# Attention and feed-forward with cached keys: each key and value tile loaded in two transfers from two queues

## The chip, the cores and the metric

The kernel runs on one core of one Trainium2 chip. Five engines share the work: PE (TensorE, the matrix engine), DVE (VectorE), ACT (ScalarE), POOL (GpSimd) and SP (SyncE, which here only issues transfers). Sixteen DMA engines carry data between the chip's main memory (HBM) and the on-chip memory (SBUF, 128 partitions). An engine works off its instructions in order, and so does a queue of transfers; between engines, and between transfers and engines, semaphores set the order. The metric is the time of one execution on the device in microseconds (us), as a median of several runs.

## The reference

One decoding step for four sequences (B = 4): a layer norm with a modulation computed from a condition c, attention of one query over 4096 cached keys and values for each of 32 heads of 128 numbers, a projection, a second modulated layer norm, and a feed-forward block with SiLU. All numbers are 32-bit floats.

```
mod = (silu(c) @ w_mod) split into sa, ca, ga, sb, cb, gb
h = layernorm(x) * (1 + ca) + sa
q = (h @ wq) split into 32 heads
scores = (q . k_cache) / sqrt(128)          # k_cache: [4, 32, 4096, 128]
p = softmax(scores)
o = (p . v_cache) @ wo                      # v_cache: [4, 32, 4096, 128]
x = x + ga * o
h = layernorm(x) * (1 + cb) + sb
x = x + gb * (silu(h @ w1) @ w2)
```

The two caches have 268 MB each; every number in them is read once, and is used in one multiplication and one addition. The weights together have 31 MB.

## The kernel before, in words

**Tiles.** The caches are worked through in N = 32 steps. A step n takes four heads of one sequence (t, b = divmod(n, 4): head group t of eight, sequence b): a key tile k_n and a value tile v_n of 128 partitions x 128 rows x 128 numbers, 8.39 MB each, 64 KB in each partition. A head's 4096 rows lie on 32 partitions, 128 rows in each, so that a tile is one stretch of HBM and each partition's 64 KB a stretch of it.

**Buffers.** All tiles and all large weights share three SBUF buffers of one tile each (the pool kv, L63), which are handed out in the order of the program: w_mod, wq, k0, v0, k1, v1, k2 and so on to k31, v31, wo, and w1 with w2. So k_{n+1} takes the buffer of v_{n-1}, and v_{n+1} that of k_n. A transfer waits at its issue until the last instruction that reads the old content is done.

**One step** (L419 to L472). GpSimd multiplies rows 0 to 39 of each partition's keys by the query (mult, L286, from a copy qw of the query in SBUF), VectorE rows 40 to 127 (from qb, the query in PSUM, the matrix engine's memory). VectorE sums both products over the 128 numbers (red, L291) to the scores. The row maxima go over PE (bmax, L299) and VectorE (negmax, L304 to L307); ScalarE takes the exponential (softexp, L313), and GpSimd puts the result in the layout that PE wants (pz, L317). Then the values: GpSimd multiplies rows 0 to 31 by their weights and adds them in halves (vmult, L329 and L333), and PE takes rows 32 to 127 (pv, L354) and later what GpSimd has left (vsum, L339). vsum of step n - 1 runs in step n: it is the last reader of v_{n-1}, and so what releases the buffer of k_{n+1}. The last reader of k_n is red. Every second step VectorE, ScalarE and PE gather the sums of two steps (gather, L368 to L378).

**Queries.** make_qb(n + 1) makes the query for the next step. At each fourth n it first builds four of them with ScalarE (L275) and PE (L277); always it copies one to SBUF with ScalarE (qw, L281).

**Order.** The program is written out by hand: each engine runs its instructions in the order of the text. All transfers are issued by SyncE through one helper (fetch, L85). Of step n, SyncE issues k_{n+1} and then v_{n+1}. Eight completion semaphores go round over the transfers, and a transfer waits for the one eight places before it to land.

**The end.** In step 31 k31 comes in two transfers by halves of its rows, wo (L426) goes into the buffer of v30, and w1 and w2 (L460) into that of k31, in ten transfers. Then follow the projection (project, L412), the second layer norm, and the feed-forward block with its last matmuls at L514.

Of the kernel before, what the change touches and what calls it, by code (L numbers as in the profile page):

```python
# [17 lines left out]
def kernel(  # L18
# [13 lines left out]
    nc = tc.nc  # L32
# [13 lines left out]
    NJ = HP * S // P  # L46
# [12 lines left out]
    N = B * NT  # L59
# [8 lines left out]
    def psum(shape, tag, bufs):  # L68
        return ps.tile(shape, F32, tag=tag, name=tag, bufs=bufs)
# [15 lines left out]
    def fetch(t, src, *cuts):  # L85
        for lo, hi in zip(cuts, cuts[1:]):
            nc.sync.dma_start(t[:, lo:hi], src[:, lo:hi])

    kt, vt = {}, {}

    def load(dst, cache, name, n, *cuts):
        t, b = divmod(n, B)
        dst[n] = Slot(f"{name}{n}").take(NJ, Dh)
        src = cache[b, HP * t : HP * (t + 1)].rearrange("h (p j) d -> (h p) j d", p=QW)
        fetch(dst[n], src, *(cuts or (0, NJ)))

    def load_k(n, *cuts):
        load(kt, kc, "k", n, *cuts)

    def load_v(n):  # L100
        load(vt, vc, "v", n)
# [169 lines left out]
    def make_qb(n):  # L271
        if n % B == 0:
            m = work.tile([P, B, Dh], F32, tag="o", name=f"qm{n}", bufs=1)
            for b in range(B):
                nc.scalar.activation(m[:, b, :], qn, AF.Copy, scale=sel[:, n + b : n + b + 1])  # L275
            p = psum([P, B, Dh], "q", 2)
            nc.tensor.matmul(p, blk.rearrange("p i x -> p (i x)"), m, start=True, stop=True)  # L277
            for b in range(B):
                qb[n + b] = p[:, b, :]
        qw[n] = work.tile([P, Dh], F32, tag="qw", name=f"qw{n}")  # L280
        nc.scalar.activation(qw[n], qb[n], AF.Copy)  # L281
# [3 lines left out]
    def mult(eng, src, n, lo, hi):  # L285
        eng.tensor_mul(  # L286
            kt[n][:, lo:hi, :], kt[n][:, lo:hi, :], src[n].unsqueeze(1).to_broadcast([P, hi - lo, Dh])
        )

    def red(n, lo, hi):  # L290
        nc.vector.tensor_reduce(sc[n][:, lo:hi], kt[n][:, lo:hi, :], axis=AX.X, op=ALU.add)  # L291

    def rowmax(n):
        nm[n] = work.tile([P, 1], F32, tag="rm", name=f"rm{n}")
        nc.vector.tensor_reduce(nm[n], sc[n], axis=AX.X, op=ALU.max)  # L295

    def bmax(n):
        p = psum([P, P], "mx", 2)
        nc.tensor.transpose(p, nm[n].to_broadcast([P, P]), ident)  # L299
        nm[n] = p  # L300

    def negmax(n):
        m = work.tile([P, HP], F32, tag="hx", name=f"hx{n}")
        nc.vector.tensor_reduce(m, nm[n].rearrange("p (i x) -> p i x", i=HP), axis=AX.X, op=ALU.max)  # L304
        nc.vector.tensor_mul(m, m, hn)
        nm[n] = work.tile([P, 1], F32, tag="nm", name=f"nm{n}")
        nc.vector.tensor_reduce(nm[n], m, axis=AX.X, op=ALU.add)  # L307

    def softexp(n):
        t, b = divmod(n, B)  # L310
        if b == 0:
            rs[t] = work.tile([P, B], F32, tag="rs", name=f"rs{t}")
        nc.scalar.activation(sc[n], sc[n], AF.Exp, bias=nm[n], accum_out=rs[t][:, b : b + 1])  # L313
        for h in range(2):
            f = first(n) if h == 0 else 0
            m = HG - f
            nc.gpsimd.tensor_mul(  # L317
                pz[h][:, f * W : HG * W].rearrange("p (g x) -> p g x", g=m)[:, :, E:].rearrange("p g (i j) -> p g i j", i=HP),
                sc[n][:, JJ * (HG * h + f) : HG * JJ * (h + 1)].rearrange("p (g j) -> p g j", j=JJ)
                .unsqueeze(2).to_broadcast([P, m, HP, JJ]),  # L320
                hm.unsqueeze(1).unsqueeze(3).to_broadcast([P, m, HP, JJ]),
            )

    def first(n):
        return NV // JJ if n < N - 2 else 0

    def vmult(n):
        if first(n):
            nc.gpsimd.tensor_mul(  # L329
                vt[n][:, :NV, :], vt[n][:, :NV, :], sc[n][:, :NV].unsqueeze(2).to_broadcast([P, NV, Dh])  # L330
            )
            for m in (NV // 2, NV // 4, JJ):
                nc.gpsimd.tensor_add(vt[n][:, :m, :], vt[n][:, :m, :], vt[n][:, m : 2 * m, :])  # L333

    def vsum(n):
        t, b = divmod(n, B)
        q, a = divmod(b, 2)
        o = (1 - a) * E
        nc.tensor.matmul(  # L339
            po[t, q][0:W, :], hs[:, o : o + W], vt[n][:, :JJ, :].rearrange("p j d -> p (j d)"),  # L340
            start=False, stop=a == 1,
        )

    def pv(n):
        t, b = divmod(n, B)
        q, a = divmod(b, 2)
        if a == 0:
            po[t, q] = psum([P, JJ * Dh], "po", 2)
        f = first(n)
        for j in range(f, NG):  # L350
            g = j % G
            h, u = divmod(j, HG)
            o = u * W + (1 - a) * E
            nc.tensor.matmul(  # L354
                po[t, q][W * g : W * (g + 1), :],
                pz[h][:, o : o + W],
                vt[n][:, JJ * j : JJ * (j + 1), :].rearrange("p j d -> p (j d)"),
                start=(a == 0 and j < f + G), stop=(a == 1 and j >= NG - G and (g > 0 or not f)),
            )
# [24 lines left out]
    def norm(t):  # L384
        p = psum([P, B], "mx", 2)
        g = part(t)
        nc.tensor.matmul(p[g], b8.rearrange("p i x -> p (i x)"), rs[t], start=True, stop=True)
        rd[t] = work.tile([P, B, QA], F32, tag="ra", name="ra", bufs=1)
        m = work.tile([P, B], F32, tag="dx", name="dx")
        nc.vector.reciprocal(m[g], p[g])  # L390
        nc.vector.tensor_mul(
            rd[t][g], m[g].unsqueeze(2).to_broadcast([W, B, QA]), dqm[g].unsqueeze(1).to_broadcast([W, B, QA])
        )

    def spread(t, lo=0, hi=B):
        g, n = part(t), hi - lo
        v = work.tile([P, n, QA, RA], F32, tag="o", name="v", bufs=1)
        nc.vector.tensor_mul(
            v[g], od[t][g, lo:hi, :].rearrange("p b (q r) -> p b q r", q=QA),
            rd[t][g, lo:hi, :].unsqueeze(3).to_broadcast([W, n, QA, RA]),  # L400
        )
        nc.vector.tensor_reduce(
            oo[t // TA][g, :, lo:hi], v[g].rearrange("p b q r -> p r b q"), axis=AX.X, op=ALU.add
        )
# [13 lines left out]
    load_v(0)  # L418
    for n in range(N):  # L419
        t, b = divmod(n, B)  # L420
        if n < N - 2:
            load_k(n + 1)
        elif n == N - 2:
            load_k(n + 1, 0, NJ // 2, NJ)
        else:
            so = Slot("wo")  # L426
            wat, wbt = so.take(RA, D), so.take(RA, D)
            fetch(wat, wav, 0, RA)
            fetch(wbt, wbv, 0, RA - 7, RA - 1, RA)
        sc[n] = work.tile([P, NJ], F32, tag="sc", name=f"sc{n}")  # L430
        if n + 1 < N:
            mult(nc.gpsimd, qw, n, 0, NA)
            mult(nc.vector, qb, n, NA, NJ)
            make_qb(n + 1)
            if n and first(n - 1):
                vsum(n - 1)
            red(n, NA, NJ)
        else:
            mid = NJ // 2
            for lo in (0, mid):  # L440
                mult(nc.gpsimd, qw, n, lo, lo + NH)
            for lo in (0, mid):
                mult(nc.vector, qb, n, lo + NH, lo + mid)
                red(n, lo + NH, lo + mid)
            for j in range(NH):
                nc.scalar.activation(kt[n][:, j, :], kt[n][:, j, :], AF.Copy, accum_out=sc[n][:, j : j + 1])
        if n + 1 < N:
            red(n, 0, NA)
        else:
            red(n, mid, mid + NH)  # L450
        rowmax(n)
        bmax(n)
        negmax(n)
        if t and b == 1:
            spread(t - 1)
        softexp(n)
        if n + 1 < N:
            load_v(n + 1)
        else:
            s2 = Slot("w12")  # L460
            w1t = s2.take(NK, F)
            w2t = s2.take(NI, D)
            fetch(w1t, w1v, 0, 3, 4)
            fetch(w2t, w2v, 0, 6, 11, NI - 1, NI)
        if b == B - 1:
            norm(t)
        vmult(n)
        pv(n)
        if n and b == 0:
            gather(t - 1, 1)  # L470
        if b == 2:
            gather(t, 0)  # L472
# [76 lines left out]
```

## Time and profile before

| | |
|---|---|
| time, median of 3 runs | 1318.7 us (1318.68 to 1318.72) |
| the profiled execution: span from the first to the last instruction | 1317.1 us |
| what lies around the span, by the median | 1.6 us |
| DVE busy | 1016.8 us (77%) |
| POOL busy | 845.4 us (64%) |
| PE busy | 376.0 us (29%) |
| ACT busy | 67.0 us (5%) |
| bytes read from HBM | 567.3 MB, 431 GB/s over the span |

For the profiled execution the page gives the span and no time of its own; the time beside it is the median of the runs. A line of the profile names the kernel's line (L286), the engine, the operation, what is written and read (out<-in) by the program's names, and how often (xcount). SPq is SyncE issuing a transfer. A view by stretches of time gives, for each stretch A:B in us from the start of the span, its length, the busy time of PE, PEld (weight loads), DVE, ACT and POOL, the granted TensorE clock, the busy share of the 16 DMA engines (1.00 is all of them, always) and GB/s.

### The profile page before, as it was taken

Reading aid. Unit: us, or ns where it says so; the run is one execution under the profiler, and the core shown is the slowest. Engines: PE = TensorE matmul, PEld = TensorE weight load, DVE = VectorE, ACT = ScalarE, POOL = GpSimd, SP = SyncE. Lnnn points to the kernel's source line nnn. Section 1 sums busy time; section 2 is a strip of 40 time slices with the busy share of each in tenths; the row PEclk is TensorE's granted clock in tenths of the full one; section 3 lists DMA queues with packets and bytes.
Section 4 is the critical chain, followed back from the end, with each engine's and each line's share of the span. In section 5 each row is a group of like instructions: output and inputs, shape, how many; then the busy total and the mean of one; then the engine's idle time right before and its main releaser. Section 6 shows DMA issues by size and latency. Waiting matters only on the chain.

```text
span 1317.1 us, 5456 instructions
## 1 busy us (share of the span) xinstructions
PE 376.0 (29%) x2090; PEld 89.8 (7%) x2090; DVE 1016.8 (77%) x353; ACT 67.0 (5%) x246; POOL 845.4 (64%) x227
## 2 busy tenths in 40 slices
PE   3421133322122332212332222233221223322056
PEld 0100000000000000000000000000000000000012
DVE  2378877777987777897777788777779877777972
ACT  1100000000000000000000000000000000000031
POOL 0236787666678766667866666876666787666650
PEclk9755666665566666556666656666655666665579
DMA  9999999999999999999999999999999999999998
GB/s 414 444 416 444 426 432 442 422 440 435 432 438 432 436 436 428 434 440 429 430 438 436 430 438 435 432 432 434 438 430 434 432 436 434 432 434 440 421 431 350
DMA packets 11209, 567.65 MB, mean 431 GB/s; under 512 B 1280, under 2 KB 1328, under 8 KB 1840
## 3 DMA queue, kind: packets, MB, share of 16 engines
q1 hardware_dynamic: 11184, 567.31, 99.6%
q8 instruction: 16, 0.26, 0.1%
q14 instruction: 9, 0.07, 0.0%
HBM read 567.30 MB, written 0.01 MB: 431 GB/s over the span
## 4 chain that ended last, share of the span: by engine, by line
DMA 37%; DVE 34%; POOL 19%; another core or an unknown queue 3%; PE 3%; issue 2%; ACT 1%; DVEq 0%; POOLq 0%; ACTq 0%
DMA k<-in_A_k_cache_dram 31%; DVE sc L291 20%; DVE k L286 14%; POOL v L333 9%; POOL v L329 8%; DMA w<-in_B_w_dram 3%; PE po L339 2%; DMA v<-in_A_v_cache_dram 2%; DMA wm<-in_A_x_dram 1%; POOL pz L317 1%; POOL k L286 1%; ACT sc L313 1%; PE mx L299 0%; DVE hx L304 0%
## 5 line engine op out<-in xcount | busy, mean ns | idle before, releaser
L291 DVE TENSOR_REDUCE sc<-k 128x88 f32<-128x11264 f32 (+1 forms) x65 | 548.9, 8484 | 1.5 <-POOL k L286 0.4
L286 DVE TENSOR_TENSOR k<-k,q 128x11264 f32<-128x11264 f32 (+1 forms) x33 | 377.4, 11435 | 199.6 <-DMA k<-in_A_k_cache_dram 199.6
L286 POOL TENSOR_TENSOR k<-k,qw 128x5120 f32<-128x5120 f32 (+1 forms) x33 | 358.6, 10868 | 39.6 <-DMA k<-in_A_k_cache_dram 39.6
L317 POOL TENSOR_TENSOR pz<-sc,hm 128x128 f32<-128x128 f32 (+1 forms) x64 | 31.5, 514 | 368.7 <-ACT sc L313 361.8
L354 PE MATMUL po<-v,pz 128*32 128x512 f32 x1568 | 241.8, 781 | 45.8 <-POOL pz L317 45.2
L333 POOL TENSOR_TENSOR v<-v 128x2048 f32<-128x2048 f32 (+2 forms) x90 | 244.8, 2719 | 7.1
L329 POOL TENSOR_TENSOR v<-v,sc 128x4096 f32<-128x4096 f32 x30 | 211.1, 7035 | 0.0
L299 PE MATMUL mx<-ident,rm 128*128 128x128 f32 x32 | 14.5, 453 | 607.7 <-DVE rm L295 607.7
L339 PE MATMUL po<-v,hs 128*32 128x512 f32 x60 | 57.5, 1061 | 231.4 <-POOL v L333 231.4
L354 PEld LDWEIGHTS po<-v,pz 128*32 128x32 f32 x1568 | 57.2, 139 | 209.1 <-issue 155.6
L299 PEld LDWEIGHTS mx<-ident,rm 128*128 128x128 f32 x32 | 5.8, 182 | 660.3 <-issue 499.2
L313 ACT ACTIVATE sc<-sc,nm 128x128 f32<-128x128 f32 x32 | 12.8, 401 | 639.4 <-DVE nm L307 639.4
L281 ACT ACTIVATE qw<-q 128x128 f32<-128x128 f32 x32 | 8.9, 277 | 460.0 <-DVE k L286 449.8
L304 DVE TENSOR_REDUCE hx<-mx 128x4 f32<-128x128 f32 x32 | 9.3, 292 | 19.7 <-PE mx L299 19.7
L339 PEld LDWEIGHTS po<-v,hs 128*32 128x32 f32 x60 | 5.5, 141 | 255.1 <-POOL v L333 255.1
L374 DVE TENSOR_REDUCE s<-o 128x128 f32<-128x512 f32 x16 | 16.6, 1039 | 0.6
L368 DVE TENSOR_TENSOR o<-po,jm 128x512 f32<-128x512 f32 x16 | 10.9, 681 | 7.6 <-PE po L354 7.6
L201 PE MATMUL q<-wm 128*32 128x512 f32 x48 | 8.8, 663 | 20.4 <-DVE wm L188 20.4
L377 ACT ACTIVATE mz<-s,am 128x128 f32<-128x128 f32 x32 | 11.1, 394 | 29.6 <-DVE s L374 29.6
L275 ACT ACTIVATE qm<-qn,sel 128x128 f32<-128x128 f32 x32 | 10.2, 390 | 46.2 <-PE od L378 46.1
L277 PE MATMUL q<-qm,blk 128*128 128x512 f32 x16 | 9.0, 645 | 12.2 <-ACT qm L275 12.2
L185 DVE SCALAR_TENSOR_TENSOR wm<-wm 128x128 f32<-128x128 f32 x1 | 0.3, 292 | 14.5 <-ACT wm L184 14.5
(99 smaller groups left out, 161.4 us busy)
## 6 DMA issues: line engine op xcount, KB each, us to landing
k<-in_A_k_cache_dram SPq DMA_DIRECT2D x2, 4096.0 KB, 22.4
wm<-in_w_mod_dram SPq DMA_DIRECT2D x1, 6144.0 KB, 17.0
wo<-in_A_wo_dram SPq DMA_DIRECT2D x1, 4096.0 KB, 26.5
w<-in_B_w_dram SPq DMA_DIRECT2D x1, 2688.0 KB, 29.2
wo<-in_A_wo_dram SPq DMA_DIRECT2D x1, 2304.0 KB, 31.4
wo<-in_A_wo_dram SPq DMA_DIRECT2D x1, 1536.0 KB, 34.6
w<-in_B_w_dram SPq DMA_DIRECT2D x1, 1536.0 KB, 34.1
w<-in_B_w_dram SPq DMA_DIRECT2D x1, 1280.0 KB, 35.0
```

The source lines that it names most:

```text
L286: eng.tensor_mul(kt[n][:, lo:hi, :], kt[n][:, lo:hi, :], src[n].unsqueeze(1).to_broadcast([P, hi - lo, Dh]))
L291: nc.vector.tensor_reduce(sc[n][:, lo:hi], kt[n][:, lo:hi, :], axis=AX.X, op=ALU.add)
L299: nc.tensor.transpose(p, nm[n].to_broadcast([P, P]), ident)
L313: nc.scalar.activation(sc[n], sc[n], AF.Exp, bias=nm[n], accum_out=rs[t][:, b : b + 1])
L317: nc.gpsimd.tensor_mul(pz[h][:, f * W : HG * W].rearrange("p (g x) -> p g x", g=m)[:, :, E:].rearrange("p g (i j) -> p g i j", i=HP), sc[n ...
L329: nc.gpsimd.tensor_mul(vt[n][:, :NV, :], vt[n][:, :NV, :], sc[n][:, :NV].unsqueeze(2).to_broadcast([P, NV, Dh]))
L333: nc.gpsimd.tensor_add(vt[n][:, :m, :], vt[n][:, :m, :], vt[n][:, m : 2 * m, :])
L339: nc.tensor.matmul(po[t, q][0:W, :], hs[:, o : o + W], vt[n][:, :JJ, :].rearrange("p j d -> p (j d)"), start=False, stop=a == 1,)
L354: nc.tensor.matmul(po[t, q][W * g : W * (g + 1), :], pz[h][:, o : o + W], vt[n][:, JJ * j : JJ * (j + 1), :].rearrange("p j d -> p (j d)") ...
L368: nc.vector.tensor_mul(o, po[t, q].rearrange("p (j d) -> p j d", j=JJ), jm.unsqueeze(2).to_broadcast([P, JJ, Dh]))
L374: nc.vector.tensor_reduce(s, o.rearrange("p j d -> p d j"), axis=AX.X, op=ALU.add)
L377: nc.scalar.activation(m[:, a, :], s, AF.Copy, scale=am[:, a : a + 1])
```

## The change

From step 1 on, each key or value transfer becomes two over all 128 partitions: a new helper fetch2 issues the first half of every partition's run on SyncE's queue and the second half on ScalarE's. k0 and v0, and all weights, stay whole on SyncE. k31, which came in two transfers, comes in four. ScalarE's halves stand in ScalarE's order of instructions, so the call of load_k moves from the head of the step to behind make_qb(n + 1), and vsum(n - 1) moves ahead of make_qb(n + 1). load_v stays where it is, behind softexp.

```diff
+    def fetch2(t, src, *cuts):
+        for lo, hi in zip(cuts, cuts[1:]):
+            mid = (lo + hi) // 2
+            nc.sync.dma_start(t[:, lo:mid], src[:, lo:mid])
+            nc.scalar.dma_start(t[:, mid:hi], src[:, mid:hi])
+
@@ def load(dst, cache, name, n, *cuts):
-        fetch(dst[n], src, *(cuts or (0, NJ)))
+        (fetch2 if n else fetch)(dst[n], src, *(cuts or (0, NJ)))
@@ for n in range(N):
-        if n < N - 2:
-            load_k(n + 1)
-        elif n == N - 2:
-            load_k(n + 1, 0, NJ // 2, NJ)
-        else:
+        if n == N - 1:
             so = Slot("wo")
...
             mult(nc.gpsimd, qw, n, 0, NA)
             mult(nc.vector, qb, n, NA, NJ)
-            make_qb(n + 1)
             if n and first(n - 1):
                 vsum(n - 1)
+            make_qb(n + 1)
+            if n < N - 2:
+                load_k(n + 1)
+            else:
+                load_k(n + 1, 0, NJ // 2, NJ)
             red(n, NA, NJ)
```

## The prediction

> **What bounds the kernel now.** I read the page first: the span, the 40 slices and the DMA queues.
>
> ```profile
> span 1317.1 us, 5456 instructions
> PE 376.0 (29%) x2090; PEld 89.8 (7%) x2090; DVE 1016.8 (77%) x353; ACT 67.0 (5%) x246; POOL 845.4 (64%) x227
> ...
> DMA  9999999999999999999999999999999999999998
> ...
> DMA packets 11209, 567.65 MB, mean 431 GB/s; under 512 B 1280, under 2 KB 1328, under 8 KB 1840
> ...
> q1 hardware_dynamic: 11184, 567.31, 99.6%
> ```
>
> The 16 DMA engines are busy in every slice, from one queue (q1, SyncE's) and without a hole. VectorE, the busiest compute engine, has 23% to spare. Next, busy time in stretches, each from one key issue to the next but one, so four tiles of 8.39 MB (128 x 128 x 128 numbers of 4 bytes).
>
> ```profile
> 262.42:339.76 77.34, 21.19 (x106) 4.75 (x106) 63.31 (x19) 3.80 (x13) 54.14 (x15) 0.59 1.00 433
> 339.76:417.01 77.25, 19.80 (x106) 4.49 (x106) 62.37 (x19) 1.96 (x7) 54.14 (x15) 0.59 1.00 434
> ...
> 649.46:726.56 77.10, 20.92 (x106) 4.73 (x106) 62.34 (x19) 1.96 (x7) 54.15 (x15) 0.59 1.00 434
> ...
> 803.74:882.12 78.38, 20.54 (x106) 4.64 (x106) 63.64 (x19) 1.96 (x7) 54.14 (x15) 0.59 1.00 433
> ```
>
> The DMA share (the column before last) is 1.00 in each, at 433 or 434 GB/s, against some 63 us of VectorE and 54 of GpSimd. A tile takes about 77.3 / 4 = 19.3 us of all 16 engines, half a tile 9.65. Then the instructions of one steady step, key tile n (start, duration, instruction, wait before it).
>
> ```profile
> 289.90 11.89 DVE L286 TENSOR_TENSOR k<-k,q 128x11264 f32<-128x11264 f32 x1 [6.27 <-DMA k<-in_A_k_cache_dram]
> ...
> 301.03 0.33 SPq L87 DMA_DIRECT2D k<-in_A_k_cache_dram  x1
> 301.82 17.28 DVE L291 TENSOR_REDUCE sc<-k 128x88 f32<-128x11264 f32 x2
> 301.88 0.28 ACT L281 ACTIVATE qw<-q 128x128 f32<-128x128 f32 x1 [19.28 <-DVE k L286]
> 319.13 0.33 SPq L87 DMA_DIRECT2D v<-in_A_v_cache_dram  x1
> ...
> 320.83 0.40 ACT L313 ACTIVATE sc<-sc,nm 128x128 f32<-128x128 f32 x1 [18.67 <-DVE nm L307]
> 321.14 0.19 ACT L313 ACTIVATION_READ_ACCUMULATOR sc<-sc,nm 128x1 f32 x1
> ...
> 322.81 0.69 ACT L377 ACTIVATE mz<-s,am 128x128 f32<-128x128 f32 x2 [1.48 <-DVE s L374]
> ...
> 328.62 11.89 DVE L286 TENSOR_TENSOR k<-k,q 128x11264 f32<-128x11264 f32 x1 [6.21 <-DMA k<-in_A_k_cache_dram]
> ...
> 331.65 1.13 PE L277 MATMUL q<-qm,blk 128*128 128x512 f32 x2 [1.37 <-ACT qm L275]
> 332.87 0.28 ACT L281 ACTIVATE qw<-q 128x128 f32<-128x128 f32 x1 [1.27 <-PE q L277]
> ...
> 337.81 1.92 PE L339 MATMUL po<-v,hs 128*32 128x512 f32 x2 [5.04 <-POOL v L333]
> 339.76 0.33 SPq L87 DMA_DIRECT2D k<-in_A_k_cache_dram  x1
> ...
> 367.21 11.89 DVE L286 TENSOR_TENSOR k<-k,q 128x11264 f32<-128x11264 f32 x1 [6.15 <-DMA k<-in_A_k_cache_dram]
> ...
> 376.36 10.99 POOL L286 TENSOR_TENSOR k<-k,qw 128x5120 f32<-128x5120 f32 x1
> ```
>
> VectorE waits over 6 us for every key tile. The tile that lands at 328.62 was issued at 301.03, 27.6 us earlier, though its own bytes need 19.3: the rest it stood behind the value tile issued before it, which lands about 328.62 - 19.3 = 309.3. So the queue holds 309.3 - 301.03 = 8.3 us of work when a key transfer joins it, and 328.62 - 319.13 = 9.5 us when a value transfer does. The kernel is bound by the rate of the DMA engines; when a transfer is issued does not matter as long as those covers are positive. Last, the end.
>
> ```profile
> 1273.55 18.91 SPq L87 DMA_DIRECT2D w<-in_B_w_dram  x6
> ...
> 1276.66 8.48 PE L354 MATMUL po<-v,pz 128*32 128x512 f32 x64 [0.58 <-DMA v<-in_A_v_cache_dram]
> ...
> 1286.86 3.62 PE L412 MATMUL acc<-wo,oo 128*4 128x512 f32 x32 [1.72 <-DMA wo<-in_A_wo_dram]
> ...
> 1311.61 2.27 PE L514 MATMUL po<-w 128*32 128x128 f32 x64 [1.45 <-DMA w<-in_B_w_dram]
> ```
>
> The last matmuls wait for the last weights. The stream of transfers therefore runs whole from the first weights to 1311.6, and 1317.1 - 1311.6 = 5.5 us of compute and the store follow. Whatever lengthens or shortens the stream is seen in full.
>
> **The change part by part.** *Transfers and packets.* The 31 value tiles from v1 on and 30 key tiles (k1 to k30) go from one transfer to two, k31 from two to four: 31 + 30 + 2 = 63 transfers more. By the page, 1280 packets under 512 B belong to 80 transfers, 16 each (the completion marks); each transfer of a tile has 128 packets of data besides, one a partition. So 63 x (128 + 16) = 9072 packets more, 567 on each of the 16 engines, with the bytes unchanged. What does one packet cost beside its bytes? Two windows of transfers, one with long packets, one late with short ones:
>
> ```profile
> DMA packets 2231, 130.22 MB, mean 434 GB/s; under 512 B 240, under 2 KB 240, under 8 KB 240
> ...
> q1 hardware_dynamic: 2226, 130.16, 100.1%
> q8 instruction: 3, 0.05, 0.1%
> ```
>
> ```profile
> DMA packets 937, 9.36 MB, mean 425 GB/s; under 512 B 104, under 2 KB 104, under 8 KB 397
> ...
> q1 hardware_dynamic: 936, 9.34, 99.9%
> q8 instruction: 1, 0.02, 0.3%
> ```
>
> The first is from 200 to 500 us, 300 x 16 = 4800 us of engine time; the second from 1287 to 1309, 352 us. With r us a MB and c us a packet, 130.22 r + 2231 c = 4800 and 9.36 r + 937 c = 352. From the first r = 36.861 - 17.13 c; put into the second, 345.02 + 776.6 c = 352, so c = 9 ns. That is an upper end, since the second window also holds an instruction fetch on another queue (0.3% of 352 = 1.06 us for 0.02 MB, which the rate r would move in 0.6 to 0.7) and cut packets at its edges. The lower end is 0: with two queues in turn, the start of one's packet may lie under the other's. I take 5 ns, a little above the middle, because only the upper end has rows. **567 x 5 ns = +2.8 us**, ends 0 and 567 x 9 = 5.1. It has no cover: the engines are at 1.00.
>
> The Trainium skill, in "DMA: Bandwidth & Descriptors", section "Why small descriptors are slow (HBM only)", gives about 3 cycles a packet on the engine's inner bus; at the 850 MHz of its section "Where 436 GB/s comes from" this is an estimate of 3.5 ns, and the sum would be +2.0 us instead of +2.8. The windows above bear out that there is such a cost, and are too coarse to tell the two prices apart.
>
> *ScalarE's issue of second halves.* 63 issues of 0.33 us (the SyncE rows) are 21 us of ScalarE, 67 us busy in 1317. The key half stands behind qw: 301.88 + 0.28 = 302.2 instead of 301.03, with 309.3 - 302.2 = 7.1 us of queue left and nothing on ScalarE until 320.83. The value half stands behind the exponential: 321.14 + 0.19 = 321.3 instead of 319.13, with 7.3 us left; behind it waits only L377 at 322.81, 1.1 us after the issue is over. Price 0. If a cover were gone in one queue, the engines would still have the other queue's half, so a late half alone costs no engine time either.
>
> *Moves.* SyncE issues only transfers, in the same order as before, so load_k's later place changes nothing there. vsum goes ahead of make_qb on PE: in each fourth step L277 (331.65) must wait for L339 to end at 339.73, so qw is ready about 339.8 + 1.1 + 0.4 = 341.3 instead of 333.2, and the key half is issued behind it. VectorE wants this q at 367.21 and GpSimd at 376.36; the value tile in transit lands about 328.62 + 19.3 = 347.9, so 6.6 us of cover remain. Price 0; without the cover, up to 1.6 us in seven steps, 11 us, if SyncE's half were hidden too, which it is not.
>
> *Start and end.* Value tile 0 and key tile 0 stay whole on SyncE.
>
> ```profile
> 58.03 11.89 DVE L286 TENSOR_TENSOR k<-k,q 128x11264 f32<-128x11264 f32 x1 [10.27 <-DMA k<-in_A_k_cache_dram]
> ...
> 69.96 0.28 ACT L281 ACTIVATE qw<-q 128x128 f32<-128x128 f32 x1 [19.67 <-DVE k L286]
> ...
> 87.26 0.33 SPq L87 DMA_DIRECT2D v<-in_A_v_cache_dram  x1
> ...
> 96.67 11.89 DVE L286 TENSOR_TENSOR k<-k,q 128x11264 f32<-128x11264 f32 x1 [7.81 <-DMA k<-in_A_k_cache_dram]
> ```
>
> ```profile
> out_dram<-w SPq DMA_DIRECT2D x1, 8.0 KB, 1.7
> ```
>
> k1's second half can go out only behind qw, at 70.3, and flows from about 72 (the smallest transfer takes 1.7 us from issue to landing). v0 then has 77.3 - 72 = 5.3 us left on SyncE. If the queues share evenly, v0 ends at 82.6, the second half at 91.3, and the first half, 5.3 us behind and now sharing with v1's second half (issued some 2 us after the first at 87.26, as in the steady step), at about 102 instead of 96.7. VectorE is then 5 us late once; it has 6 us of wait a step to make up, and v1's first half stands in SyncE's queue from 87.26 on, so the engines never idle. Price 0 in the total. At the end wo and w stay on SyncE behind v31's first half; PE has v31 at 1276.66 and next waits for wo at 1286.86, having been done with v31 at 1285.1, so up to 1.7 us of lag between the halves is covered.
>
> The sum against the profiled execution: 1317.1 + 2.8 = 1319.9 us of span. The median of the runs, 1318.7, is 1.6 above that span, so **1321.5 us**, with 1318.7 to 1323.8 from the two ends.
>
> **The rivals.** *No cost to be seen.* The added packets start under the other queue's, nothing else moves: 1318.7. For it: the engines stay fed and bytes are equal. Against it: short packets ran at 425 GB/s and long ones at 434, in one queue. The Trainium skill ("DMA: Bandwidth & Descriptors", section "Issuing engines are not separate DMA queues") says the same of queues: all issuers share the 16 engines and save only issue time, which by the SyncE rows is hidden here; by that rule there is no gain to expect.
>
> *Faster: two queues close the gaps that one leaves.* The 62 tiles cost each engine 62 x 9 = 558 packets now; if these 5 ns vanish and the new ones cost nothing, -2.8 us: 1315.9. It decides from the point where packets of two queues overlap wholly. For it: 77.10 us for four tiles in one row and 77.4 in the mean. Against it: a share of 1.00 leaves no idle time, and the stretches differ by hiccups (78.38) that a queue doesn't cause.
>
> *Changing queues is dear.* An engine would alternate between two queues some 16 times a tile, about 1000 times in all. The one such change that the rows show, the instruction fetch, cost 1.06 us for what r moves in 0.6 to 0.7, so 0.4 us; at that price 400 us more, 1720. But that time lies in the fetch's own packet, which speaks for a slow target rather than a dear change. A few cycles, say 10 ns, would give +10 and with the packets 1331.
>
> *A half comes late.* If ScalarE's halves lose their 7 us of cover, and SyncE's run dry with them, each step loses what is missing: 0.3 us in 30 steps is 9 us, 1330. Against it: SyncE's issues keep covers of 8.3 and 9.5 us.
>
> **How the numbers follow.** Chances: the forecast 0.48, no cost 0.24, faster 0.10, dear change 0.14, late half 0.04. About 0.2%, 2.6 us, is what a measurement of this kernel tells from no change; that is 1321.3, in the middle of the forecast's own range of 1318.7 to 1323.8. Of the forecast I count 0.30 as slower and 0.18 as the same; with the others: slower 0.30 + 0.14 + 0.04 = 0.48, same 0.18 + 0.24 = 0.42, faster 0.10. The range of 8 in 10 leaves out the dear change beyond 10 ns and half of the faster case: 1316 to 1331.
>
> **What would show it.** Two data queues of some 307 and 260 MB (half of 62 tiles' 520 MB moves); about 20,280 packets; DMA share still 1.00; stretches of four tiles longer by 36 x 5 ns = 0.18 us, near 77.5; VectorE's second key tile at about 102; its later waits for keys again over 5 us; the last matmuls 2.8 us later, at 1314.4. I am wrong if the stretches shrink (the gaps were real and close), if they grow by a microsecond or more (changing queues costs), or if the DMA slices show holes (a half is late).

## The result, and the profile after

The changed kernel takes **1321.72 us** (median of 12 runs, 1321.53 to 1322.32) against 1318.78 us (12 runs, 1318.61 to 1319.11) for the kernel before: 2.9 us more, a ratio of 1.0022 with a 95% interval of 1.0015 to 1.003. The profiled execution took 1321.56 us with a span of 1319.8 us, 2.7 us longer than the span before. The page of the changed kernel:

```profile
span 1319.8 us, 5635 instructions
PE 384.6 (29%) x2090; PEld 91.6 (7%) x2090; DVE 1016.8 (77%) x353; ACT 67.0 (5%) x246; POOL 845.0 (64%) x227
...
DMA  9999999999999999999999999999999999999998
...
DMA packets 20282, 567.66 MB, mean 430 GB/s; under 512 B 2288, under 2 KB 2336, under 8 KB 2848
...
q1 hardware_dynamic: 11184, 307.26, 54.0%
q10 hardware_dynamic: 9072, 260.05, 45.7%
```

The second queue (q10, ScalarE's) carries the second halves, 260 MB. The engines are as full as before, the bytes are the same, and the compute engines do the same work. Only the packets have grown, by 20282 - 11209 = 9073, one of them an instruction fetch. Where the time lies is seen in one long stretch, from the issue of k4 to that of k31, first before and then after (columns as in the prediction: length, five busy times, clock, DMA share, GB/s):

```profile
185.31:1229.75 1044.44, 279.95 (x1429) 63.05 (x1429) 849.27 (x244) 37.26 (x130) 730.91 (x190) 0.59 1.00 434
```

```profile
186.65:1233.70 1047.05, 289.60 (x1431) 64.99 (x1431) 849.64 (x244) 37.51 (x131) 730.65 (x190) 0.59 1.00 433
```

The 27 steps take 2.61 us more, at a DMA share of 1.00 in both; the rest of the program accounts for 0.1 us of the 2.7 (1.34 us more ahead of this stretch, 1.25 less behind it). A pair of steps (four tiles) goes from 1044.44 / 13.5 = 77.37 to 77.56 us. One steady step after, with both queues' issues:

```profile
302.88 0.33 SPq L92 DMA_DIRECT2D k<-in_A_k_cache_dram  x1
303.71 17.28 DVE L297 TENSOR_REDUCE sc<-k 128x88 f32<-128x11264 f32 x2
303.71 0.28 ACT L287 ACTIVATE qw<-q 128x128 f32<-128x128 f32 x1 [19.25 <-DVE k L292]
303.80 0.33 ACTq L93 DMA_DIRECT2D k<-in_A_k_cache_dram  x1
321.02 0.33 SPq L92 DMA_DIRECT2D v<-in_A_v_cache_dram  x1
...
322.84 0.33 ACTq L93 DMA_DIRECT2D v<-in_A_v_cache_dram  x1
...
330.56 11.89 DVE L292 TENSOR_TENSOR k<-k,q 128x11264 f32<-128x11264 f32 x1 [6.27 <-DMA k<-in_A_k_cache_dram]
...
369.14 11.89 DVE L292 TENSOR_TENSOR k<-k,q 128x11264 f32<-128x11264 f32 x1 [6.14 <-DMA k<-in_A_k_cache_dram]
```

ScalarE's halves leave 0.9 us (keys) and 1.8 us (values) behind SyncE's, long before the tile ahead of them has landed, and VectorE waits for keys 6.1 to 6.3 us, as before. At the end the last matmuls start 2.58 us later than the 1311.61 before:

```profile
1314.19 2.26 PE L520 MATMUL po<-w 128*32 128x128 f32 x64 [1.28 <-DMA w<-in_B_w_dram]
```

### The profile page after: what moved, and what is told of

The parts are those of the page before. It is cut to its first block, busy times and chain, and to the rows that moved or that the text cites. A ratio compares the mean times of both kernels' runs of the same rounds, so it can differ in the third digit from the quotient of the medians.

```text
span 1319.8 us, 5635 instructions
## 1 busy us (share of the span) xinstructions
PE 384.6 (29%) x2090; PEld 91.6 (7%) x2090; DVE 1016.8 (77%) x353; ACT 67.0 (5%) x246; POOL 845.0 (64%) x227
## 2 busy tenths in 40 slices
DMA packets 20282, 567.66 MB, mean 430 GB/s; under 512 B 2288, under 2 KB 2336, under 8 KB 2848
## 3 DMA queue, kind: packets, MB, share of 16 engines
q1 hardware_dynamic: 11184, 307.26, 54.0%
q10 hardware_dynamic: 9072, 260.05, 45.7%
## 4 chain that ended last, share of the span: by engine, by line
POOL 54%; issue 26%; DMA 10%; DVE 6%; PE 2%; another core or an unknown queue 1%; ACT 0%; POOLq 0%; SPq 0%; ACTq 0%; DVEq 0%
POOL k L292 22%; POOL v L339 15%; POOL v L335 15%; DMA k<-in_A_k_cache_dram 4%; DVE k L292 3%; DVE sc L297 3%; DMA w<-in_B_w_dram 3%; POOL pz L323 2%; DMA v<-in_A_v_cache_dram 2%; DMA wm<-in_c_dram 1%; PE q L207 1%; PE q L256 1%; PE q L219 0%; PE po L520 0%
## 5 line engine op out<-in xcount | busy, mean ns | idle before, releaser
L283 PE MATMUL q<-qm,blk 128*128 128x512 f32 x16 | 15.3, 1055 | 2.6 <-ACT qm L281 2.6
```

## The experiments

Three causes could give 2.9 us: the packets themselves, going from one queue to the other, or the late halves and moved calls on ScalarE. Each time below stands against the kernel before as it ran beside it: 1318.8 us for both halves on SyncE's queue, only the moved calls, quarters on SyncE's queue and the cut by partitions on two queues; 1318.72 us for quarters on both queues, the short packets and the next two cuts by partitions; 1318.86 us for the last.

**Both halves on SyncE's queue.** The second queue is taken away, the packets stay.

```diff
             nc.sync.dma_start(t[:, lo:mid], src[:, lo:mid])
-            nc.scalar.dma_start(t[:, mid:hi], src[:, mid:hi])
+            nc.sync.dma_start(t[:, mid:hi], src[:, mid:hi])
```

> The changed kernel with both halves of every tile issued by SyncE, so the same 9072 added packets and no second data queue. Packet theory (each packet costs some 5 ns beside its bytes, whatever its queue): 2.8 us over the kernel before, some 1321.6 us, as the changed kernel. Queue theory (an engine pays for going from one queue to the other): no change, 1318.8 us. Theory of the late half or the moved calls on ScalarE: no change, 1318.8 us, as ScalarE issues nothing. The second key tile should reach VectorE near 96.9 us again, as one queue keeps order.

Measured: 1321.71 us (11 runs, 1321.29 to 1322.31), ratio 1.0021 (1.0013 to 1.003). Its page and its second key tile on VectorE:

```profile
DMA packets 20283, 567.67 MB, mean 430 GB/s; under 512 B 2288, under 2 KB 2336, under 8 KB 2848
...
q1 hardware_dynamic: 20256, 567.31, 99.7%
```

```profile
96.74 11.89 DVE L292 TENSOR_TENSOR k<-k,q 128x11264 f32<-128x11264 f32 x1 [7.82 <-DMA k<-in_A_k_cache_dram]
```

The time is that of the changed kernel to 0.01 us, though there is one queue and ScalarE issues nothing. So neither the second queue nor ScalarE's part costs or gains anything that can be measured; the cut in two does it alone.

**Only the moved calls.**

```diff
-        (fetch2 if n else fetch)(dst[n], src, *(cuts or (0, NJ)))
+        fetch(dst[n], src, *(cuts or (0, NJ)))
```

> Only the moved calls of the change (vsum ahead of make_qb, load_k behind it); every tile comes whole on SyncE as before. Packet theory and queue theory: no change, 1318.8 us, the page's packets at 11209 again. Theory of the moves: part or all of the 2.9 us, up to 1321.7 us.

Measured: 1318.76 us (11 runs, 1318.68 to 1319.14), ratio 0.9999 (0.9991 to 1.0008), with 11209 packets. The moves cost nothing that can be measured.

**Quarters on SyncE's queue.** The packets of data of each tile are doubled once more.

```diff
-            mid = (lo + hi) // 2
-            nc.sync.dma_start(t[:, lo:mid], src[:, lo:mid])
-            nc.scalar.dma_start(t[:, mid:hi], src[:, mid:hi])
+            q = (hi - lo) // (4 if hi - lo == NJ else 2)
+            for a in range(lo, hi, q):
+                nc.sync.dma_start(t[:, a : a + q], src[:, a : a + q])
```

> Each tile in four transfers by each partition's run, all on SyncE (the last key tile in four, as in the changed kernel): 31 x 3 + 30 x 3 + 2 = 185 transfers more than before, 185 x 144 = 26640 packets, 1665 an engine. Packet theory: 1665 x 5 ns = 8.3 us, 1327.1 us. Queue theory and late-half theory: no change, 1318.8 us; a cost of the transfer and not of its packets would give 185/63 of 2.9 us, 8.5 us, as well.

Measured: 1327.19 us (5 runs, 1327.12 to 1327.64), ratio 1.0063 (1.0051 to 1.0075).

```profile
DMA packets 37853, 567.69 MB, mean 428 GB/s; under 512 B 4240, under 2 KB 4288, under 8 KB 4800
...
q1 hardware_dynamic: 37824, 567.32, 100.0%
```

37824 - 11184 = 26640 packets more, 1665 an engine, and 8.4 us: 5.0 ns each. The halves gave 2.9 us for 567, 5.1 ns each. The cost goes with the number of pieces.

**Quarters on both queues.**

```diff
             mid = (lo + hi) // 2
-            nc.sync.dma_start(t[:, lo:mid], src[:, lo:mid])
-            nc.scalar.dma_start(t[:, mid:hi], src[:, mid:hi])
+            q = (hi - lo) // (4 if hi - lo == NJ else 2)
+            for a in range(lo, hi, q):
+                eng = nc.sync if a < mid else nc.scalar
+                eng.dma_start(t[:, a : a + q], src[:, a : a + q])
```

> Each tile in four transfers by each partition's run, the first two on SyncE, the last two on ScalarE (the last key tile in four): the packets of the quarters on one queue (26640 more than before), but an engine goes from queue to queue at each of them. Packet theory with the 5 ns that the quarters on one queue gave (8.4 us for 1665 packets): 1327.2 us, the same as those. Queue theory: more than 1327.2 us, by twice the changes of the changed kernel.

Measured: 1327.46 us (5 runs, 1327.23 to 1328.18), ratio 1.0068 (1.0054 to 1.0081). Within the intervals this is the quarters on one queue; the 0.3 us between them would be 0.3 / 1984 = 0.15 ns for each change of queue if it were one (31 tiles of each kind, 32 packets a tile on an engine). The queue theory falls twice.

**Short packets in whole transfers.** So far transfers and packets grew together. Here only packets of data do.

```diff
-        (fetch2 if n else fetch)(dst[n], src, *(cuts or (0, NJ)))
+        if 0 < n < N - 1:
+            nc.sync.dma_start(
+                dst[n].rearrange("q (a c) d -> q a (c d)", a=4),
+                src.rearrange("q (a c) d -> q a (c d)", a=4)[:, ::-1, :],
+            )
+        else:
+            fetch(dst[n], src, *(cuts or (0, NJ)))
```

> The tiles of steps 1 to 30 come whole, one transfer each on SyncE as before, but with each partition's run in four pieces taken in reverse order (rows 96 to 127, 64 to 95, 32 to 63, 0 to 31; keys and values alike, so that sums go over the same pairs): four packets of 16 KB in place of one of 64 KB, no transfer and no completion mark more. 60 tiles x 24 = 1440 packets more on each engine. If the price is the packet's (8.4 us for 1665): 7.2 us, 1326.0 us. If it is the transfer's (8.4 us for 185 transfers): 1318.8 us.

Measured: 1325.51 us (5 runs, 1325.45 to 1325.79), ratio 1.0051 (1.0038 to 1.0064).

```profile
span 1323.7 us, 5456 instructions
...
DMA packets 34249, 567.65 MB, mean 429 GB/s; under 512 B 1280, under 2 KB 1328, under 8 KB 1840
```

The instructions (5456) and the completion marks (1280 packets under 512 B) are those of the kernel before; 34249 - 11209 = 23040 packets of data are new, 1440 an engine. They cost 1325.51 - 1318.72 = 6.8 us, 4.7 ns a packet (3.5 to 5.9 by the interval). So the price is mostly the packet's, not the transfer's. What the quarters cost beyond that is 8.4 - 1480 x 4.7 ns = 1.4 us for 185 transfers, and the halves 2.9 - 504 x 4.7 ns = 0.5 us for 63: some 8 ns for each transfer on each engine, its completion mark among it. Remainders this small lie within the intervals.

The packet records of the traces give the price more sharply. They do not name the engine, so a packet is paired here with the only one that starts within 10 ns of its end, between 200 and 1200 us. From start to start it takes 2414.13 ns for 64 KB (the kernel before), 1209.41 ns for 32 KB (the changed kernel, and both halves on one queue) and 607.06 ns for 16 KB (quarters on one queue and on two, and the short packets). Twice 1209.41 less 2414.13 is 4.7 ns, and so is twice 607.06 less 1209.41: each packet costs 4.7 ns beside its bytes. In the changed kernel 10237 of 10251 such pairs go from one queue to the other, at the same 1209.41 ns, so a change of queue costs nothing. A completion mark between two packets adds 6 ns (median). By these two prices the halves come to 504 x 4.7 + 63 x 6 ns = 2.7 us and the quarters to 8.1 us, where 2.9 and 8.4 were measured.

**Cut by partitions.** Meant as a second test of the queues: two queues without new packets of data.

```diff
-            nc.sync.dma_start(t[:, lo:mid], src[:, lo:mid])
-            nc.scalar.dma_start(t[:, mid:hi], src[:, mid:hi])
+            nc.sync.dma_start(t[: P // 2, lo:hi], src[: P // 2, lo:hi])
+            nc.scalar.dma_start(t[P // 2 :, lo:hi], src[P // 2 :, lo:hi])
```

> Each tile in two transfers over two queues as in the changed kernel, but cut by partitions (0 to 63 on SyncE, 64 to 127 on ScalarE) instead of by each partition's run: packets of data stay 64 KB and as many as before, only the 63 x 16 completion marks are added, 63 an engine. Packet theory: 63 x 5 ns = 0.3 us, 1319.1 us. Queue theory: an engine changes queue half as often as in the changed kernel, so half of its 2.9 us, 1320.2 us or more. Late-half theory: as the changed kernel, 1321.7 us. The second key tile should reach VectorE one or two 64 KB packets (2.4 us each) late, 99.3 to 101.8 us.

Measured: 2538 us (6 runs, 2475 to 2562), 1.88 to 1.94 times the kernel before. No theory had this. From its transfers between 600 and 700 us:

```profile
DMA packets 389, 21.17 MB, mean 212 GB/s; under 512 B 66, under 2 KB 66, under 8 KB 66
...
q1 hardware_dynamic: 196, 10.68, 49.9%
q10 hardware_dynamic: 193, 10.49, 48.8%
```

The engines are all but busy (98.7%) and move half of what they did. 1600 us of engine time x 0.987 over 389 - 66 = 323 packets of data are 4.9 us for each 64 KB packet. The kernel before takes 2.4 us, 3200 us of engine time over 1484 - 160 = 1324 such packets between 300 and 500 us:

```profile
DMA packets 1484, 86.61 MB, mean 433 GB/s; under 512 B 160, under 2 KB 160, under 8 KB 160
```

This run says nothing on queues, and it asked for three more.

Both halves by partitions on SyncE:

```diff
-            mid = (lo + hi) // 2
-            nc.sync.dma_start(t[:, lo:mid], src[:, lo:mid])
-            nc.scalar.dma_start(t[:, mid:hi], src[:, mid:hi])
+            for a, b in ((0, P // 2), (P // 2, P)):
+                nc.sync.dma_start(t[a:b, lo:hi], src[a:b, lo:hi])
```

> The cut by partitions again, 0 to 63 and then 64 to 127, but both on SyncE: no second queue. If it was the two queues that made the cut by partitions take 2538 us: 1319.1 us, the engines at 434 GB/s. If 64 neighbouring partitions by themselves take 16 engines at half rate (packets of 4.8 us instead of 2.4): some 215 GB/s in the steady stretches and about 2500 us again.

Measured: 2622 us (2 runs), ratio 1.9879 (1.9843 to 1.9915). One queue is as slow as two: the cut is to blame.

Middle and ends, on SyncE (W = 32; the lines replaced are the same three, here and in the last cut):

```diff
+            for a, b in ((W, P - W), (0, W), (P - W, P)):
+                nc.sync.dma_start(t[a:b, lo:hi], src[a:b, lo:hi])
```

> Each tile from step 1 on in three transfers on SyncE: partitions 32 to 95, then 0 to 31, then 96 to 127. If what counts is which partitions the 16 engines write at a time, and partitions 0 to 63 share one half of the ways into SBUF and 64 to 127 the other, then the middle goes at the full rate and the ends at half: 9.65 + 19.3 = 29 us a tile, 62 x 9.65 = 598 us over the kernel before, some 1917 us. If any transfer of fewer than 128 partitions is slow: about 2500 us. If neither: 1319.4 us.

Measured: 2561 us (2 runs, 2518 and 2604). Its transfers between 1000 and 1300 us:

```profile
DMA packets 1367, 64.73 MB, mean 216 GB/s; under 512 B 376, under 2 KB 376, under 8 KB 376
...
q1 hardware_dynamic: 1363, 64.69, 100.0%
```

Neither 1917 us nor a middle at full rate is left in the steady steps, so the theory of two halves of SBUF, as put, falls. But the first tile cut in this way, k1, does what the theory says. Its middle moves in the first of these stretches, its ends in the second (columns as before; a packet counts whole in the stretch in which it starts, so that a share can pass 1.00):

```profile
75.00:84.60 9.60, 0.00 (x0) 0.00 (x0) 9.60 (x2) 0.00 (x0) 0.00 (x0) 0.50 1.00 430
84.60:104.30 19.70, 8.11 (x49) 1.98 (x49) 3.49 (x5) 0.49 (x2) 14.71 (x5) 0.67 1.02 216
```

That is 29.3 us for the tile, where the theory had 29. In the kernel with both halves by partitions on SyncE, the first half of k1 (partitions 0 to 63, as many bytes as the middle) has half that rate from its start:

```profile
75.00:84.60 9.60, 0.00 (x0) 0.00 (x0) 9.60 (x2) 0.00 (x0) 0.00 (x0) 0.50 1.03 218
```

So a transfer of 64 partitions is not slow as such; it depends on which 64. In the later tiles the middle loses its rate: between 300 and 500 us at least three in four of the 64 KB packets take over 4.5 us, against 2.4 at full rate. Perhaps the engines no longer go from middle to ends together; no run shows why.

Halves by partitions, each with its reads spread over the whole tile: partitions 0 to 63 take every second 64 KB run of the tile's stretch of HBM, 64 to 127 the others.

```diff
+            for a in range(2):
+                nc.sync.dma_start(t[a * P // 2 : (a + 1) * P // 2, lo:hi], src[a::2, lo:hi])
```

> [...] Heads get each other's rows, so the sums are not those of the reference; instructions, bytes, packets and partitions are those of the cut by partitions on one queue. If that cut is slow by where it reads in HBM: 434 GB/s and some 1319 us. If it is slow by where it writes in SBUF: some 215 GB/s and 2500 to 2600 us again.

Measured: 2618 us (2 runs), ratio 1.985 (1.9765 to 1.9936), and between 1000 and 1300 us:

```profile
DMA packets 1195, 62.43 MB, mean 208 GB/s; under 512 B 240, under 2 KB 240, under 8 KB 240
```

Where in the tile each half reads makes no difference here. In its steady steps every cut by partitions tried here runs at half rate. That spreading the reads did not help, and that a middle of 64 partitions started at full rate, speaks for the writing side: for which partitions are written at the same time. The profile does not show how such a transfer is dealt out to the engines, so the cause stays open.

## Why the prediction was right, and where it was not

*Packets and their price.* Right. 9072 added packets were counted and 9072 came. Each was put at 5 ns, between 0 and 9; the halves on one queue give 5.1 ns, the packet records 4.7 for a packet of data and 6 for a completion mark. 2.8 us were forecast, 2.9 came. That 5 came so near was partly luck: it rested on no row of its own, only on the middle of two bounds. The upper bound of 9 from the late window was too high, and held other things too, as the text said; with a lower end of 0 the two windows could not bear out by themselves that there is a cost.

*No cover.* Right. The stretch of 27 steps grew by 2.61 us for 54 tiles of 9 packets more, 5.4 ns each, and the last matmuls start 2.58 us later. Four tiles take 77.56 us, where 77.37 + 0.18 = 77.55 follows from the step as forecast. The agreement is closer than such a stretch can show: k4 is issued 1.34 us later than before and k31 3.95, so its ends scatter by about a microsecond.

*ScalarE's issues and the moves at nothing.* Right, and shown: the halves on one queue remove ScalarE's part and give back 0.01 us, the moved calls alone cost nothing measurable. The key halves leave at 303.80, 0.9 us behind SyncE's, and in the fourth step at 343.49 against 341.64.

*The start.* The mechanism was right, its size wrong. k1 was put at about 102; it came to VectorE at 99.35. The step that failed is "flows from about 72": the 1.7 us from issue to landing of the small store at the end, in an idle queue, were taken for the time to the first packet. ScalarE's issue and the two windows around its first packets:

```profile
70.28 0.39 ACTq L93 DMA_DIRECT2D k<-in_A_k_cache_dram  x1
```

```profile
q10 hardware_dynamic: 2, 0.07, 15.2%
```

```profile
q10 hardware_dynamic: 14, 0.46, 106.1%
q1 hardware_dynamic: 1, 0.07, 15.1%
```

```profile
99.35 11.89 DVE L292 TENSOR_TENSOR k<-k,q 128x11264 f32<-128x11264 f32 x1 [10.24 <-DMA k<-in_A_k_cache_dram]
```

The first two packets of the new queue start between 74 and 75 us, the next 14 between 75 and 76: some 4 to 5 us from the issue. Sixteen more 64 KB packets of SyncE's queue had started between 72.2 and 73.3 us; presumably each engine first ended what it had already taken up. By then v0, which would have ended alone near 77.6, had 2 to 3 us left, so the second half got that far ahead of the first, and not 5.3: k0 is 0.25 us later here (58.28), and 99.35 - 96.67 - 0.25 = 2.4 us is the lead. As forecast it costs nothing in the total: the halves on one queue have k1 at 96.74 and the same time.

*The end.* The sum was not touched, but "the stream runs to 1311.6" was loosely read: the wait that ends there is for a piece before the last. The last weights (256 KB) of the kernel before:

```profile
1292.13 0.33 SPq L87 DMA_DIRECT2D w<-in_B_w_dram  x1
```

```profile
w<-in_B_w_dram SPq DMA_DIRECT2D x1, 256.0 KB, 21.3
```

They were issued at 1292.13 and landed 21.3 us later, at 1313.4. They wait behind everything else in SyncE's queue, so the whole 2.6 us came through all the same.

*The rivals.* "No cost to be seen" fell: short packets in whole transfers cost 6.8 us. "Faster" fell with it: two queues hide nothing of a packet's cost, as one queue and two give the same time at halves and at quarters. "Changing queues is dear" fell: 1209.41 ns from packet to packet with a change and without. The instruction fetch, which held an engine longer than its bytes need, was no measure of it. "A half comes late" had no case. The Trainium skill's price, about 3 cycles or by estimate 3.5 ns ("DMA: Bandwidth & Descriptors", section "Why small descriptors are slow (HBM only)"), lies below the 4.7 ns of the packet records.

## What to carry to other kernels

When the DMA share is 1.00 in every steady stretch, a second issuing queue has nothing to fill, and each cut of a transfer adds packets whose small fixed price (here some 5 ns on the engine that moves it, 0.4% of a 32 KB packet) comes straight into the time. Count the packets of such a change from the profile before asking which queue they go on. And a cut that keeps the packets but leaves partitions out of a transfer is a different thing: measure it before using it.

## What the runs showed of the hardware that was not expected

- Tiles cut by partitions moved 208 to 216 GB/s in the steady steps, against 433 for transfers over all 128, with the engines busy all the time; in the cut on two queues a 64 KB packet took 4.9 us for 2.4. It was so for two neighbouring halves on one queue and on two, for a middle and two ends, and with the reads in HBM spread out. Yet partitions 32 to 95 of the first tile so cut moved at 430 GB/s, and partitions 0 to 63 at 218. The cause was not settled.
- Two queues with work share the 16 engines packet by packet in turn, and at no cost. In the changed kernel between 300 and 500 us each has half of the packets and of the bytes:

```profile
DMA packets 2962, 86.54 MB, mean 433 GB/s; under 512 B 320, under 2 KB 320, under 8 KB 320
...
q1 hardware_dynamic: 1483, 43.35, 50.2%
q10 hardware_dynamic: 1477, 43.16, 50.0%
```

- A packet's price was the same 4.7 ns at 64, 32 and 16 KB. Reading a partition's run in four pieces in reverse order cost that price and no more: 607.06 ns a packet, as in the quarters.
